# State-space layer and token mixer on one core: a third of the parameter chain to GpSimd, x's later rows issued earlier, two weight loads held back

## The chip, the cores and the metric

The kernel runs on one core of one Trainium2 chip. The metric is device time in microseconds (us) of one execution; lower is better. The engines are named as in the profile: PE (TensorE, with PEld for its weight loads), DVE (VectorE), ACT (ScalarE), POOL (GpSimd), and SP (SyncE), which issues most DMAs. POOL issues some DMAs too, on a queue of its own.

## The reference

A sequence x of 2048 tokens and 448 channels passes two blocks, each behind a layer norm whose scale and shift come from a conditioning vector c. Block A is a state-space convolution (S4D), computed by FFT; block B is a two-layer MLP over the token axis. Cut to what matters:

```python
def _A_ref(u, log_A_real, A_imag, C_real, C_imag, log_dt, D_skip):
    dt = jnp.exp(log_dt)
    A = -jnp.exp(log_A_real) + 1j * A_imag          # (448, 256)
    C = (C_real + 1j * C_imag) * dt[:, None]
    P = jnp.exp((A * dt[:, None])[:, :, None] * pos[None, None, :])
    K = 2.0 * jnp.einsum("dn,dnl->dl", C, P).real    # kernel, 448 x 2048
    y = jnp.fft.irfft(rfft(u_t, 2 * L) * rfft(K, 2 * L))[:, :, :L]
    return y + u * D_skip

mod = (silu(c) @ w_mod).reshape(1, 6, 1, 448)
sa, ca, ga, sb, cb, gb = ...                         # the six rows of mod
h = layernorm(x) * (1 + ca) + sa
x = x + ga * _A_ref(h, ...)
h = layernorm(x) * (1 + cb) + sb
x = x + gb * (w2.T @ gelu(w1.T @ layernorm(h) + b1) + b2)   # over tokens
```

## The kernel before

Everything is fp32. The convolution kernel K is built per step of 8 channels and 256 states: there are 56 steps (two for each of 28 groups of 16 channels), and the program runs them in sets of eight. A set begins with `window(s)`, s = 0, 8, 16, ..., 48, which does the part that needs the exponential's function table for all eight steps. Then come the eight steps themselves, which need the sine.

In `window`, for each of eight e: PE multiplies the exponent rows `lex` with the table `tab` into PSUM (`xe`, `xg`), and ACT takes their exponentials (`mag`). In each step, PE multiplies the phase rows `lph` (`st_phase`), ACT takes two absolute values and four sines (`ab`, `gs`, `xe`, `xg`), POOL makes the two halves of `G` (L679, L680), DVE the four parts of `E` (L681 to L687), and PE multiplies E and G into the kernel (`kg`, L710). For two later steps POOL makes `w` and `m` (L654, L656).

The rows `lex` and `lph` are parameters: from C, A and dt of each channel, magnitudes and phases are worked out, each split into two fp32r numbers `hl` (a rounded copy and the rest), and stored to a DRAM scratch `pars[q]`, from which SP loads a group's rows. q counts four blocks of 128 channels. Block 0 is done ahead of everything (`first_chain`), straight on 128 x 256 tiles. Blocks 1 to 3 are a Python generator, `chain(q)`: each `yield` ends one DVE instruction, and `more(n)` emits the next n of them at places that `WPACE` (in a set) and `pace` (in a step) name. So block 1's second half is emitted within the set of step 8, block 2's within the set of step 16, and block 3's along the steps behind. In those two sets DVE also empties PSUM for the FFT of u (`u_rows`, tile `yt`, L556): PE's `pu` waits for a free PSUM buffer, and the exponent matmuls are queued behind it.

x's rows come in three `x_load` calls, issued by POOL: rows 0 to 3 and 4 to 7 in `first_chain`, 8 to 15 behind step 0. `u_stats(r)` takes the mean and variance of row group r on DVE (L527, L528): 0 to 3 in the set of step 0, the others between the steps, by `late_rows`. All 16 are needed by ACT's `rs` (L462) and DVE's `nm` (L532) at the beginning of the set of step 8, and these by the normalised rows that `u_rows` multiplies.

The modulation rows 4 and 5 of `w_mod` are loaded late, into a part of `yks[1]` (`late_load`, called at steps 34 and 36 and read at steps 40 and 48).

The order of PE, ACT, DVE and POOL is the order of the code (a manual schedule). SP's order is made by a scheduler, which puts each DMA where its inputs and its buffer are expected to be ready. Each engine runs its queue in order. Behind step 55 come the inverse transform, the second layer norm and the MLP, in which PE is busy almost throughout.

Of the kernel before, what the change touches and what calls it, by code (L numbers as in the profile page):

```python
# [11 lines left out]
F32 = mybir.dt.float32  # L12
# [3 lines left out]
ALU = mybir.AluOpType  # L16
# [205 lines left out]
def tile_adaln_s4d_mixer(ctx, tc, i, out):  # L222
# [21 lines left out]
    with ExitStack() as es:  # L244
# [128 lines left out]
        def chain(q):  # L373


            w = N if q < 3 else P
            cr, ci, a, aim = (raws[q][nm][:, 0:w] for nm in ("A_C_real", "A_C_imag", "A_log_A_real", "A_A_imag"))
            xa, ya, s, t, u, ph, p64 = (
                qp.tile([P, N], F32, tag=nm, name=nm)[:, 0:w] for nm in ("xa", "ya", "s", "t", "u", "ph", "p64")
            )  # L380

            def split(src, to):
                hl = qp.tile([P, 2, N], F32R, tag="hl", name="hl", bufs=3)[:, :, 0:w]
                V.tensor_copy(hl[:, 0], src)
                yield
                tt(hl[:, 1], src, hl[:, 0].bitcast(F32), ALU.subtract)
# [10 lines left out]
            S.activation(xa, cr, AF.Abs, scale=0.5)  # L397
# [10 lines left out]
            ts(t, s, 2.0**-40, 2.0**80, ALU.is_lt, ALU.mult)  # L408
# [6 lines left out]
            ya = u  # L415
            yield from split(a, [(0, 1), (1, 1)])
            stt(s, t, -80 * math.log(2.0) / 2.0**80, s, ALU.mult, ALU.add)
            yield
            tt(s, ya, s, ALU.add)
            yield  # L420
            yield from split(s, [(2, 1)])
            yield "exponents"

            ts(ph, aim, dt4[:, q : q + 1], None, ALU.mult)
            yield
            ts(u, ph, MAGIC, MAGIC, ALU.add, ALU.subtract)
            yield
            tt(ph, ph, u, ALU.subtract)
            yield
            yield from split(ph, [(0, 0)])  # L430

            ts(u, ph, MAGIC / 128, MAGIC / 128, ALU.add, ALU.subtract)
            yield
            tt(p64, ph, u, ALU.subtract)
            yield
            yield from split(p64, [(1, 0)])

            ts(u, cr, 0.0, 0.5, ALU.is_ge, ALU.subtract)
            yield
            tt(xa, xa, u, ALU.mult)  # L440
            yield
            ts(u, ci, 0.0, 0.5, ALU.is_ge, ALU.subtract)
            yield
            stt(xa, xa, 0.5, u, ALU.add, ALU.mult)
            yield
            stt(xa, ph, 63.0, xa, ALU.mult, ALU.add)
            yield
            ts(u, xa, MAGIC, MAGIC, ALU.add, ALU.subtract)
            yield
            tt(xa, xa, u, ALU.subtract)  # L450
            yield
            yield from split(xa, [(2, 0)])
        def logs(root=False):

            if tmp:
# [43 lines left out]

        def late_load(k):  # L500
            a = (3456, 5376)[k - 4]
            wms[k] = late_room()[:, a : a + 4 * D].rearrange("p (q d) -> p q d", q=4)
            nc.sync.dma_start(wms[k], i["w_mod"][:, k * D : (k + 1) * D].rearrange("(q p) d -> p q d", p=PP))

# [353 lines left out]
        def first_chain():  # L858
# [79 lines left out]
            tt(xa, xa, u, ALU.subtract)  # L938
            store(ha, (0, 1), (1, 1))
            hl = split(G, p64)  # L940
            x_load(4, 4, G)
            direct(hl, lph, 64, 0)
            hc = split(V, xa)
            direct(hc, lph, 96, 0)
# [59 lines left out]
        def window(s):  # L1004
# [9 lines left out]
            for e in range(BATCH):  # L1014
                st_exp(s + e)

                if e + 1 < BATCH:
                    st_exponents(s + e + 1)
                else:
                    st_phase(s)  # L1020
                mellow()
                if s == 8 and e == 0:
                    tt(mod[1], mod[1], mod[2], ALU.mult)
                flush(dve)
                flush(act)
# [12 lines left out]
                if s in (8, 16):  # L1038
                    some(u_rows, rows, (1, 1, 1, 1, 1, 0, 0, 1)[e])
                elif s == 24 and e != 5:  # L1040
                    some(u_cols, cols, 1)

                if s == 32 and e == 2:
                    nc.sync.dma_start(t0, i["T0"].rearrange("p (j m) -> p j m", j=2))
                if s == 32 and e == 5:
                    pc_load(1)
                if s >= 40 and e == 2:
                    piece(False)
                if s >= 32 and e == 4:
                    piece(pieces[0] < NP, V)  # L1050
                if s == 0 and e in (4, 5):
                    st_mag2(e - 4)
                elif s and (e < 2 or s >= 32):
                    st_mag2(s + e)
                if s == 8 and e == 0:
                    u_norm(e + 2)
                if s == 0 and e == 3:
                    for r in range(4):
                        dsk_copy(r)
            if s == 0:  # L1060

                S.activation(one, one, AF.Sin)

        WPACE = [[0] * 8, [0, 2, 3, 4, 5, 5, 5, 5], [0, 5, 4, 4, 4, 4, 4, 4], [2] * 8]
        pace = [2] * 32
        mod_steps = {2: (1, 0), 3: (1, 1), 6: (2, 0, 1), 12: (0, 0), 13: (0, 1)}
        late_rows = {0: (4, 5), 3: (6, 7), 5: (8, 9, 10), 6: (11, 12, 13), 7: (14, 15)}
        tail = NHALF + 3  # L1070
        for s in range(tail):
            if s == 32:
# [402 lines left out]
```

## Time and profile before

| | |
|---|---|
| median of three runs | 683.14 us (681.51 to 683.85) |
| profiled execution | 685.58 us, span 683.7 us |
| PE busy | 614.2 us, 90% |
| PEld busy | 455.9 us, 67% |
| DVE busy | 446.5 us, 65% |
| ACT busy | 438.8 us, 64% |
| POOL busy | 267.6 us, 39% |
| granted TensorE clock | 0.970 |
| DMA | 121.14 MB, mean 177 GB/s |

Shares over the whole span say little here, since the stages have different bounds. On the time axis of the profile the parameters of block 0 and the set of step 0 take up to about 31 us, steps 0 to 7 up to 66, the set of step 8 up to 88, steps 8 to 15 up to 122, the set of step 16 up to 138, the set of step 32 lies at 221 to 235, the last step ends at about 344, and the MLP fills the rest. In a row of the order of time stand the start, the length, the engine, the line, the instruction with its output and inputs, and in brackets the engine's idle time before it with what ended that. A row of a table by stretches has the stretch, its length, and the busy time of PE, PEld, DVE, ACT and POOL (with counts), then the granted clock, the busy share of the DMA engines and GB/s.

### The profile page before, as it was taken

The numbers are of one execution on the slowest core, as the hardware profiler recorded it, in microseconds if no ns is written. First come the engines' busy times: TensorE is split into PE (matmuls) and PEld (weight loads), VectorE is DVE, ScalarE is ACT, GpSimd is POOL, SyncE is SP. The second block draws the span as 40 slices with busy tenths as digits, with TensorE's granted clock in tenths as the row PEclk, the third lists the DMA queues.
The fourth block names the chain that finished last, engine by engine and source line by source line (L and its number), as shares of the span: only waits on it lengthen the run. The fifth ranks groups of instructions, "written<-read, shape, count | busy, mean of one in ns | idle before, by whom it ended". The sixth has DMA issues, their size and how long they took to land. (4 is left out here: it accounts for less than half of the span.)

```text
span 683.7 us, 18268 instructions
## 1 busy us (share of the span) xinstructions
PE 614.2 (90%) x7180; PEld 455.9 (67%) x7180; DVE 446.5 (65%) x870; ACT 438.8 (64%) x880; POOL 267.6 (39%) x322
## 2 busy tenths in 40 slices
PE   0686789879988799999989899999999999999997
PEld 0354445435535456565667677779999999999996
DVE  7399798987689396885967587777422454443331
ACT  5787699879989799999945588877322322222220
POOL 6297468368369689898848100000000000000000
PEclk9999779989999899999999999999999999999999
DMA  8882455568896955344349799946674345555530
GB/s 182 237 181 75 174 173 188 194 208 261 264 288 191 206 124 179 99 138 131 99 140 314 231 256 257 243 127 198 167 213 135 95 141 168 165 162 170 167 119 28
DMA packets 106211, 121.14 MB, mean 177 GB/s; under 512 B 13098, under 2 KB 94718, under 8 KB 105998
## 3 DMA queue, kind: packets, MB, share of 16 engines
q1 hardware_dynamic: 104942, 114.72, 58.2%
q0 software_dynamic: 1184, 5.26, 3.4%
q8 instruction: 57, 0.93, 0.6%
q14 instruction: 28, 0.23, 0.1%
HBM read 84.59 MB, written 34.87 MB: 175 GB/s over the span
## 5 line engine op out<-in xcount | busy, mean ns | idle before, releaser
L207 ACT CAST whi<-w 128x896 fp32r<-128x896 f32 x64 | 59.7, 938 | 133.7 <-PE o L1442 84.7
L679 POOL TENSOR_TENSOR G<-mag,gs 128x512 f32<-128x512 f32 x56 | 72.1, 1288 | 66.9 <-ACT gs L675 66.7
L216 DVE TENSOR_TENSOR wlo<-w,whi 128x896 fp32r<-128x896 f32 x64 | 68.0, 1086 | 40.3 <-ACT whi L207 31.0
L1372 PE MATMUL acc<-h3h,whi 128*128 128x448 f32 x224 | 83.2, 372 | 1.2 <-ACT h3h L1277 1.2
L1374 PE MATMUL acc<-h3h,wlo 128*128 128x448 f32 x224 | 81.9, 366 | 0.0
L1373 PE MATMUL acc<-h3l,whi 128*128 128x448 f32 x224 | 81.6, 364 | 0.2 <-DVE h3l L1280 0.2
L1441 PE MATMUL o<-uh,whi 128*128 128x448 f32 x224 | 81.3, 363 | 0.0
L1443 PE MATMUL o<-uh,wlo 128*128 128x448 f32 x224 | 81.2, 362 | 0.0
L1442 PE MATMUL o<-ul,whi 128*128 128x448 f32 x224 | 80.6, 360 | 0.0
L710 PEld LDWEIGHTS kg<-E,G 128*32 128x32 f32 x3584 | 56.2, 114 | 31.5 <-issue 14.5
L627 PE MATMUL xg<-tab,lph 64*128 64x512 f32 x112 | 63.9, 572 | 12.6 <-DVE E L687 4.7
L680 POOL TENSOR_TENSOR G<-mag,gs 128x512 f32<-128x512 f32 x56 | 71.8, 1281 | 0.0
L710 PE MATMUL kg<-E,G 128*32 128x64 f32 x3584 | 66.1, 227 | 3.8 <-POOL G L680 1.7
L627 PE MATMUL xe<-tab,lph 64*128 64x512 f32 x112 | 63.7, 572 | 4.9 <-ACT gs L676 2.1
L1445 DVE SCALAR_TENSOR_TENSOR y<-o,b,mod 128x448 f32<-128x448 f32 x16 | 11.0, 685 | 80.3 <-PE o L1443 80.3
L656 POOL TENSOR_TENSOR m<-mag,w 128x512 f32<-128x512 f32 x56 | 59.7, 1065 | 4.4
L681 DVE TENSOR_TENSOR E<-m,xe 128x512 f32<-128x512 f32 x56 | 38.2, 682 | 26.0 <-ACT xe L674 21.9
L627 PE MATMUL xe<-tab,lex 64*128 64x512 f32 x56 | 31.1, 569 | 23.7 <-DMA lex<-wm 17.3
L1372 PEld LDWEIGHTS acc<-h3h,whi 128*128 128x128 f32 x224 | 42.4, 190 | 13.3 <-ACT h L1282 4.2
L1374 PEld LDWEIGHTS acc<-h3h,wlo 128*128 128x128 f32 x224 | 42.5, 190 | 3.3
L1373 PEld LDWEIGHTS acc<-h3l,whi 128*128 128x128 f32 x224 | 42.3, 189 | 3.4 <-DVE h3l L1280 0.5
L638 ACT ACTIVATE mag<-xe 128x512 f32<-128x512 f32 x56 | 35.5, 635 | 13.9 <-PE xe L627 5.7
(239 smaller groups left out, 1442.8 us busy)
## 6 DMA issues: line engine op xcount, KB each, us to landing
w<-in_B_w_dram SPq DMA_DIRECT2D x64, 224.0 KB
w<-in_B_w_dram SPq DMA_DIRECT2D x32, 448.0 KB
yu_d<-yt SPq DMA_DIRECT2D x16, 448.0 KB
yi<-yu_d SPq DMA_DIRECT2D x16, 448.0 KB
us_d<-uo SPq DMA_DIRECT2D x16, 448.0 KB
u<-us_d SPq DMA_DIRECT2D x32, 224.0 KB
v_d<-vt SPq DMA_DIRECT2D x32, 224.0 KB
vt<-v_d SPq DMA_DIRECT2D x14, 448.0 KB
```

The source lines that it names most:

```text
L207: self.nc.scalar.copy(hi, w)
L216: eng.tensor_tensor(lo, w, hi.bitcast(F32), ALU.subtract)
L627: T.matmul(out[k], lhs[r], rhs[r], start=start, stop=stop)
L679: G.tensor_tensor(Gt[:, 1], mg_, v32(sg), ALU.mult)
L680: G.tensor_tensor(Gt[:, 0], mg_, v32(cg_), ALU.mult)
L710: T.matmul(kgs[g][32 * q : 32 * q + 32, m], Gt[:, c, d], E[:, c, d], start=h == 0 and c == 0 and m == 0, stop=h == 1 and c == 1, skip_grou ...
L1372: nc.tensor.matmul(acc[f], hi[:, fs], h3h[:, r], start=r == 0, stop=False)
L1373: nc.tensor.matmul(acc[f], hi[:, fs], h3l[:, r], start=False, stop=False)
L1374: nc.tensor.matmul(acc[f], lo[:, fs], h3h[:, r], start=False, stop=r == 15)
L1441: nc.tensor.matmul(o, hi[:, ks], uh[kh][:, k], start=kh == 0 and k == 0, stop=False)
L1442: nc.tensor.matmul(o, hi[:, ks], ul[kh][:, k], start=False, stop=False)
L1443: nc.tensor.matmul(o, lo[:, ks], uh[kh][:, k], start=False, stop=kh == 1 and k == 6)
```

## The change

Three things are changed.

The phases' part of `chain(q)` for q = 1 and 2 goes from DVE to POOL (`E = G if q < 3 else V`). One instruction with two operations (63 times ph, plus xa) becomes two, so that 14 instructions leave DVE and 15 come to POOL in each of the two sets; the four sign instructions stay on DVE and come earlier. Block 3 stays on DVE with one instruction more.

x's rows 4 to 7 and 8 to 15 are issued by POOL within the set of step 0, behind the `m` of step 0 and of step 1. The statistics of rows 4 to 7 go to the end of that set, those of 8 to 15 into steps 2 to 6. Two modulation matmul groups go from steps 2 and 3 to 3 and 4.

`late_load` first writes one column of its room on DVE, and the load waits for that write, so it can't start before steps 34 and 36.

```diff
-            def split(src, to):
+            def split(src, to, eng=V):
...
+            E = G if q < 3 else V
+            r = ya
+            def turn(v):
+                E.tensor_scalar(r, v, MAGIC, MAGIC, ALU.add, ALU.subtract)
+                yield
+                E.tensor_tensor(v, v, r, ALU.subtract)
+                yield
+            E.tensor_scalar(ph, aim, dt4[:, q : q + 1], None, ALU.mult)
+            yield
+            yield from turn(ph)
+            yield from split(ph, [(0, 0)], E)
             ts(u, cr, 0.0, 0.5, ALU.is_ge, ALU.subtract)
...
-            stt(xa, ph, 63.0, xa, ALU.mult, ALU.add)
...
+            E.tensor_scalar(r, ph, MAGIC / 128, MAGIC / 128, ALU.add, ALU.subtract)
+            yield
+            E.tensor_tensor(p64, ph, r, ALU.subtract)
+            yield
+            yield from split(p64, [(1, 0)], E)
+            E.tensor_scalar(r, ph, 63.0, None, ALU.mult)
+            yield
+            E.tensor_tensor(xa, xa, r, ALU.add)
+            yield
+            yield from turn(xa)
+            yield from split(xa, [(2, 0)], E)
...
         def late_load(k):
+            V.memset(late_room()[:, a : a + 1], 0.0)
...
             hl = split(G, p64)
-            x_load(4, 4, G)
...
                 if s == 0 and e in (4, 5):
                     st_mag2(e - 4)
+                    x_load((4, 8)[e - 4], (4, 8)[e - 4], G)
...
             if s == 0:
+                for r in range(4, 8):
+                    u_stats(r)
...
-        WPACE = [[0] * 8, [0, 2, 3, 4, 5, 5, 5, 5], [0, 5, 4, 4, 4, 4, 4, 4], [2] * 8]
+        WPACE = [[0] * 8, [2, 2, 3, 4, 5, 5, 5, 5], [0, 5, 4, 4, 4, 4, 4, 4], [2] * 8]
-        mod_steps = {2: (1, 0), 3: (1, 1), 6: (2, 0, 1), 12: (0, 0), 13: (0, 1)}
-        late_rows = {0: (4, 5), 3: (6, 7), 5: (8, 9, 10), 6: (11, 12, 13), 7: (14, 15)}
+        mod_steps = {3: (1, 0), 4: (1, 1), 6: (2, 0, 1), 12: (0, 0), 13: (0, 1)}
+        late_rows = {2: (8,), 3: (9, 10), 4: (11, 12), 5: (13,), 6: (14, 15)}
...
-            if s == 0:
-                x_load(8, 8, G)
```

The order of the instructions shows what moves. First POOL, from block 0's last cast to the end of step 0; `xt` holds x's rows, and a row of 32x1792 x4 is rows 4 to 7, of 32x3584 x4 rows 8 to 15. Before:

```order
L869 CAST wm_79<-p_186 128x256
L870 TENSOR_TENSOR wm_79<-p_186,wm_79 128x256
L305 DMA xt<-in_A_u_dram 32x1792 x4
L477 COPY dsk<-dskr 1x112 x4
L654 TENSOR_TENSOR w<-mag 128x16
L656 TENSOR_TENSOR m_329<-mag,w 128x512
L654 TENSOR_TENSOR w<-mag 128x16
L656 TENSOR_TENSOR m_343<-mag,w 128x512
L679 TENSOR_TENSOR G<-mag,gs 128x512
L680 TENSOR_TENSOR G<-mag,gs 128x512
L305 DMA xt<-in_A_u_dram 32x3584 x4
```

And the same place on POOL after:

```order
L875 TENSOR_TENSOR wm_79<-p_186,wm_79 128x256
L481 COPY dsk<-dskr 1x112 x4
L659 TENSOR_TENSOR w<-mag 128x16
L661 TENSOR_TENSOR m_325<-mag,w 128x512
L305 DMA xt<-in_A_u_dram 32x1792 x4
L659 TENSOR_TENSOR w<-mag 128x16
L661 TENSOR_TENSOR m_343<-mag,w 128x512
L305 DMA xt<-in_A_u_dram 32x3584 x4
L684 TENSOR_TENSOR G<-mag,gs 128x512
```

Rows 4 to 7 are issued later, behind the first `m`, and rows 8 to 15 earlier, ahead of the first `G`.

Next DVE in the set of step 8, from block 1's last magnitude to the first `E` of step 8; `yt` is the emptying of PSUM that PE's `pu` waits for. Before (the rows from p to the sign instructions left out):

```order
L386 TENSOR_TENSOR hl<-s,hl 128x256
L424 TENSOR_SCALAR ph<-A_A_imag,dt_172 128x256
L426 TENSOR_SCALAR u<-ph 128x256
L556 TENSOR_TENSOR yt<-pu,mod_105 128x448 x2
L428 TENSOR_TENSOR ph<-ph,u 128x256
L384 CAST hl<-ph 128x256
L386 TENSOR_TENSOR hl<-ph,hl 128x256
L432 TENSOR_SCALAR u<-ph 128x256
L434 TENSOR_TENSOR p_414<-ph,u 128x256
L556 TENSOR_TENSOR yt<-pu,mod_105 128x448 x2
```

And DVE after, from the same instruction to the first `E`:

```order
L386 TENSOR_TENSOR hl<-s,hl 128x256
L734 TENSOR_TENSOR ks<-ks,dsk 128x4
L561 TENSOR_TENSOR yt<-pu,mod_105 128x448 x4
L436 TENSOR_SCALAR u<-A_C_real 128x256
L438 TENSOR_TENSOR xa<-xa,u 128x256
L440 TENSOR_SCALAR u<-A_C_imag 128x256
L442 SCALAR_TENSOR_TENSOR xa<-xa,u 128x256
L561 TENSOR_TENSOR yt<-pu,mod_105 128x448 x4
L686 TENSOR_TENSOR E<-m_979,xe 128x16x32
```

Between the sets of `yt` only the four sign instructions are left; the fourteen others now stand on POOL, between the set's last `m` and the first `G` of step 8. The set of step 16 changes in the same way.

Last SP around the late weight loads (`yk<-in_w_mod`), in and behind the set of step 32. Before:

```order
L779 DMA si<-in_SI_dram 128x512
L503 DMA yk_3470<-in_w_mod_dram 112x4x448
L774 DMA u<-us_d 128x448
L503 DMA yk_3470<-in_w_mod_dram 112x4x448
L785 DMA yk_1115<-in_SI_dram 128x384
L774 DMA u<-us_d 128x448
L613 DMA lex_146<-pars_59 32x256
L617 DMA lex_146<-pars_59 64x1x256
```

And SP after, from the last of the next set's `lex` loads on:

```order
L618 DMA lex_149<-pars_59 32x256
L622 DMA lex_149<-pars_59 64x1x256
L779 DMA u<-us_d 128x448
L784 DMA si<-in_SI_dram 128x512
L846 DMA v_d<-vt 128x2x224
L618 DMA lph_144<-pars_59 32x256
L622 DMA lph_144<-pars_59 64x1x256
L790 DMA yk_1117<-in_SI_dram 128x384
L508 DMA yk_3473<-in_w_mod_dram 112x4x448
```

The first of the two loads now stands behind the four `lex` pairs, and the second follows some transfers later, each waiting for its write on DVE.

More of the change, by code (lines that the diff above doesn't have):

```diff
@@ L380, in chain @@
             )
-            def split(src, to):
+            def split(src, to, eng=V):
                 hl = qp.tile([P, 2, N], F32R, tag="hl", name="hl", bufs=3)[:, :, 0:w]
-                V.tensor_copy(hl[:, 0], src)
+                eng.tensor_copy(hl[:, 0], src)
                 yield
-                tt(hl[:, 1], src, hl[:, 0].bitcast(F32), ALU.subtract)
+                eng.tensor_tensor(hl[:, 1], src, hl[:, 0].bitcast(F32), ALU.subtract)
                 for k, v in to:
@@ L418, in chain @@
             yield
-            tt(s, ya, s, ALU.add)
+            tt(s, u, s, ALU.add)
             yield
@@ L422, in chain @@
             yield "exponents"
-            ts(ph, aim, dt4[:, q : q + 1], None, ALU.mult)
-            yield
[L426 to L436, printed above, removed]
+            E = G if q < 3 else V
[6 more added lines that the diff above has]
+            E.tensor_scalar(ph, aim, dt4[:, q : q + 1], None, ALU.mult)
+            yield
+            yield from turn(ph)
+            yield from split(ph, [(0, 0)], E)
             ts(u, cr, 0.0, 0.5, ALU.is_ge, ALU.subtract)
@@ L445, in chain @@
             yield
-            stt(xa, ph, 63.0, xa, ALU.mult, ALU.add)
+            E.tensor_scalar(r, ph, MAGIC / 128, MAGIC / 128, ALU.add, ALU.subtract)
             yield
-            ts(u, xa, MAGIC, MAGIC, ALU.add, ALU.subtract)
+            E.tensor_tensor(p64, ph, r, ALU.subtract)
             yield
-            tt(xa, xa, u, ALU.subtract)
+            yield from split(p64, [(1, 0)], E)
+            E.tensor_scalar(r, ph, 63.0, None, ALU.mult)
             yield
-            yield from split(xa, [(2, 0)])
+            E.tensor_tensor(xa, xa, r, ALU.add)
+            yield
+            yield from turn(xa)
+            yield from split(xa, [(2, 0)], E)
         def logs(root=False):
```

1 line of the change is left out of this document (removed).

## The prediction

> **What bounds the kernel now.** I read busy time by stretches first, one stretch for each place that the change touches, then the order of time of each engine there, then who waited for whom.
>
> ```profile
> 33.00:64.00 31.00, 24.47 (x450) 14.29 (x450) 30.43 (x55) 26.42 (x54) 30.05 (x33) 0.94 0.62 150
> 69.00:88.00 19.00, 14.99 (x191) 8.28 (x184) 14.41 (x38) 11.88 (x25) 7.23 (x10) 0.80 0.56 188
> 125.00:138.00 13.00, 10.88 (x171) 6.03 (x167) 11.71 (x29) 11.24 (x24) 2.68 (x4) 1.00 0.64 234
> 222.00:236.00 14.00, 10.30 (x202) 6.30 (x205) 3.91 (x9) 10.49 (x21) 10.70 (x17) 0.79 1.03 232
> ```
>
> After the stretch and its length stand the busy times of PE, PEld, DVE, ACT and POOL, then granted clock, DMA share, GB/s. Steps 0 to 7 (33 to 64): DVE and POOL are both full, 30.4 and 30.1 of 31 us. Set of step 8 (69 to 88) and set of step 16 (125 to 138): DVE is the busiest or nearly, POOL almost idle. Set of step 32 (222 to 236): DMA is full and every engine has gaps. The stages behind 236 us have none of the changed work, so I take a gain ahead of them as passed on to the end.
>
> **Steps 0 to 7.** In order of time, DVE, ACT, POOL:
>
> ```profile
> 32.96 0.69 DVE L681 TENSOR_TENSOR E<-m,xe 128x512 f32<-128x512 f32 x1 [11.46 <-ACT xe L674]
> 57.47 0.59 DVE L527 BATCH_NORM_STATS2 st<-xt 128x6 f32<-128x448 f32 x1
> 58.20 0.59 DVE L527 BATCH_NORM_STATS2 st<-xt 128x6 f32<-128x448 f32 x1
> 68.15 0.31 ACT L462 ACTIVATE rs<-mv,small_t 128x16 f32<-128x16 f32 x1 [2.38 <-DVE mv L528]
> 68.74 0.18 DVE L532 TENSOR_TENSOR nm<-rs 128x16 f32<-128x16 f32 x1 [0.62 <-ACT rs L463]
> 35.89 2.00 POOL L305 DMA_DIRECT2D xt<-in_A_u_dram  x4
> ```
>
> One row's statistics take 58.20 - 57.47 = 0.73 us. Rows 4 to 7 leave this stretch for DVE's idle 11.46 us ahead of 32.96: 4 x 0.73 = 2.9 us. The last rows' statistics now stand ahead of step 7's products, so rs no longer makes DVE wait: 0.62. POOL's issue at 35.89 goes ahead of its first G, into idle time: 2.0. As DVE is the later one, nm could start 3.5 us earlier.
>
> Against that stand the transfers. Rows 4 to 7 (4 x 224 KB) now go behind POOL's first m instead of ahead of it, and rows 8 to 15 (4 x 448 KB = 1.84 MB) behind its second m, ahead of the first G, instead of at 35.89. There they meet:
>
> ```profile
> 23.32 2.04 SPq L884 DMA_DIRECT2D pars<-wm  x4
> 27.79 0.37 SPq L613 DMA_DIRECT2D lph<-pars  x1
> 34.28 0.42 ACT L397 ACTIVATE xa<-A_C_real 128x256 f32<-128x256 f32 x1
> 34.50 0.46 PE L627 MATMUL xe<-tab,lph 64*128 64x512 f32 x1 [1.96 <-ACT xg L677]
> 42.37 0.68 DVE L681 TENSOR_TENSOR E<-m,xe 128x512 f32<-128x512 f32 x1
> 39.00 0.60 ACT L674 ACTIVATE xe<-xe 128x512 f32<-128x512 f32 x1
> 22.00:28.00 6.00, 5.75 (x15) 2.97 (x13) 0.00 (x0) 5.57 (x12) 1.29 (x2) 1.00 0.88 304
> 28.00:36.00 8.00, 5.21 (x21) 3.13 (x21) 2.88 (x5) 7.97 (x17) 2.55 (x3) 0.97 0.66 168
> q1 hardware_dynamic: 104942, 114.72, 58.2%
> q0 software_dynamic: 1184, 5.26, 3.4%
> ```
>
> The lph load at 27.79 reads what the stores at 23.32 write, and step 2's matmul at 34.50 reads lph. If the 1.84 MB go wholly ahead of those stores, at 304 GB/s, lph comes 6.0 us later; if behind, not at all. ACT's xa at 34.28, whose input SP issues between the two, is exposed in the same way, and all of ACT queues behind it. Step 2's sine ran at 39.00 to 39.60 and its reader at 42.37: 2.8 us of slack. Worst case 6.0 - 2.8 = 3.2 late, of which DVE wins back rows 6 and 7 (1.45) and 0.62: +1.1. Ends: -3.5 and +1.1. The mean packets of POOL's queue are 4.4 KB against 1.1 KB of SP's, so I lean to part of the delay: -1.8.
>
> The Trainium skill's page DMA: Bandwidth & Descriptors (Queues, rings and completion order) says that an engine takes turns between queues packet by packet; with larger packets on POOL's queue this would give the +1.1 end, 679.0 in all, against 675.6 by my lean. No run yet shows which.
>
> Ahead of step 0, in the first set:
>
> ```profile
> 21.60 0.79 PE L627 MATMUL xg<-tab,lex 64*128 64x512 f32 x1 [3.52 <-DMA lex<-wm]
> ```
>
> This wait for lex loses the competition of rows 4 to 7, but the lph of step 0, which SP issues behind it and which ends the same set, gains it. Ends: -3.5 (the wait gone) and +3.5 (the same wait moved to lph); I take -0.5, near the middle, because the transfers change places rather than go away. Rows 4 to 7 themselves: POOL issues them near the start of DVE's 11.46 idle us, of which 2.9 are now used, so they have about 8.5 us to land. Two modulation matmul groups move one or two steps later and the pace of the set of step 8 starts two instructions earlier: the same work in steps with the same bound, at 0. Together: **-2.3**.
>
> **The set of step 8.** The steps that leave DVE, first and last, then who waits for DVE, and POOL:
>
> ```profile
> 80.56 0.34 DVE L424 TENSOR_SCALAR ph<-A_A_imag,dt 128x256 f32<-128x256 f32 x1
> 88.86 0.42 DVE L386 TENSOR_TENSOR hl<-xa,hl 128x256 fp32r<-128x256 f32 x1
> PE y L748 <- DVE yt L556: 1.8, 2, 1.3
> PE pu L553 <- DVE yt L556: 1.1, 2, 0.7
> 91.38 1.27 POOL L679 TENSOR_TENSOR G<-mag,gs 128x512 f32<-128x512 f32 x1 [14.13 <-ACT gs L675]
> 12.75 0.52 POOL L869 CAST wm<-ph 128x256 fp32r<-128x256 f32 x1 [2.48 <-DVE ph L927]
> 13.35 0.77 POOL L870 TENSOR_TENSOR wm<-ph,wm 128x256 fp32r<-128x256 f32 x1
> 74.30 1.62 POOL L543 TENSOR_SCALAR xt<-xt,rs,nm 128x448 f32<-128x448 f32 x2
> ```
>
> Fourteen DVE instructions of 0.28 to 0.43 leave this set, 5.0 us. PE waited for DVE's yt 1.8 + 1.1 = 2.9 us; the exponent matmuls and ACT's mag queue behind that. So the gain lies between 0 and 5.0, bounded in practice by PE's 2.9: I take **-2.0**, since the next paragraph eats some.
>
> POOL gets fifteen instructions: 7 two-input x 0.77, 3 casts x 0.52, 5 scalar x 0.46 (1.62/2 x 256/448) = 9.3 us, behind the set's last m and ahead of G at 91.38. The cover is POOL's 14.13 idle us; if it were gone, G would be late and ACT would wait for its gs buffers. DVE supplies xa half-way through the set, before POOL's eleventh instruction. The stores that these fifteen feed are read from step 16 on, with steps 8 to 15 between.
>
> DVE and POOL disturb each other:
>
> ```profile
> 44.76 1.98 DVE L408 TENSOR_SCALAR t<-s 128x256 f32<-128x256 f32 x1
> 102.98 0.48 DVE L408 TENSOR_SCALAR t<-s 128x256 f32<-128x256 f32 x1
> 127.78 1.27 DVE L417 SCALAR_TENSOR_TENSOR s<-t,s 128x256 f32<-128x256 f32 x1
> 77.90 0.41 DVE L417 SCALAR_TENSOR_TENSOR s<-t,s 128x256 f32<-128x256 f32 x1
> ```
>
> The long ones stand beside a POOL tensor instruction, the short ones do not (an m beside the 1.27). Six such DVE instructions remain beside the moved chain; at most 0.77 each is 4.6 us, almost what left.
>
> The Trainium skill, SBUF — State Buffer (SBUF: two separate sides), states this as an exclusive lock that also takes DVE instructions with two SBUF inputs; the 1.27 against 0.41 agrees. By it alone the set would gain some 0.4 us, and the whole change come to 678.2 (rival 2).
>
> **The set of step 16**, the same chain:
>
> ```profile
> PE pu L553 <- DVE yt L556: 1.5, 2, 1.0
> PE y L748 <- DVE yt L556: 0.6, 1, 0.6
> 141.17 0.69 DVE L681 TENSOR_TENSOR E<-m,xe 128x512 f32<-128x512 f32 x1 [1.16 <-ACT xe L674]
> 141.65 1.27 POOL L679 TENSOR_TENSOR G<-mag,gs 128x512 f32<-128x512 f32 x1 [12.89 <-ACT gs L675]
> ```
>
> PE's waits are 2.1, and DVE already waits 1.16 for ACT at the end, so less is to be had: between 0 and 2.1, **-1.2**. POOL's cover is 12.89 against 9.3. The third group's chain stays on DVE with one instruction of 128x128 more: 0.3 us, hidden, at 0.
>
> **The weight loads.**
>
> ```profile
> 223.34 0.34 SPq L503 DMA_DIRECT2D yk<-in_w_mod_dram  x1
> 229.14 0.50 PE L627 MATMUL xe<-tab,lex 64*128 64x512 f32 x1 [2.97 <-issue]
> 231.67 0.60 ACT L638 ACTIVATE mag<-xe 128x512 f32<-128x512 f32 x1 [0.91 <-issue]
> ```
>
> Two loads of 784 KB, the first at 223.34 and one right after, go into a full DMA (share 1.03 above), and PE, then ACT, stand still 2.97 and 0.91 us for nothing that the profile shows. I read it as instructions fetched late through the same DMA engines. A memset on DVE now releases each load at steps 34 and 36 (cost 0 to 1.5 us each, as 1.98 against 0.48; I take 0, DVE has gaps there), and on SP they stand behind lex and u loads, which so come earlier. Behind the waiting load SP holds si and v_d transfers for one step at most. Its readers come at steps 40 and 48. Ends: 0 and -3.9. The si and u loads that also fill DMA there stay, so I take the half, **-2.0**.
>
> **Sum.** -2.3 - 2.0 - 1.2 - 2.0 = -7.5 us. The profiled execution took 685.58 us (span 683.7), the median is 683.14: I forecast 683.1 - 7.5 = **675.6**. What a measurement can tell from no change is 0.3%, 2.0 us.
>
> **Rivals.**
> 1. The x transfers hold up SP's: first term +1.1 instead of -2.3, 679.0. For it: packet sizes and the lph chain; against it: DMA is at 0.66 from 28 to 36.
> 2. DVE and POOL block each other: both sets gain 0.4 and 0.2, 678.2. For it: 1.98 against 0.48. With rival 1, 681.6: no change.
> 3. The loads' hold does nothing, the stall comes from si and u loads: 677.6.
> 4. Slower: POOL's chain outlasts its cover. At P us per instruction G is late by 15P - 14.1 and 15P - 12.9, and the steps behind it wait; both sets' gains are then gone, and with the other two terms the sum is 30P - 27.0 - 4.3. It turns positive at 1.04 and reaches +2 at 1.11; at G's own 1.27 it is +6.8, 689.9. Against it: G is twice as wide, and the narrow rows say 0.46 to 0.77, so it would take blocking by DVE at nearly every instruction.
> 5. All terms at their good ends, -3.5 - 3.5 - 2.9 - 2.1 - 3.9 = -15.9: 667.2.
>
> **Chances.** Forecast (673 to 678) 0.46, rival 1 0.14, rival 2 0.10, rival 3 0.08, rivals 1 and 2 together 0.10, rival 4 0.05, towards 5 (below 673) 0.07. Faster 0.46 + 0.14 + 0.10 + 0.08 + 0.07 = 0.85, same 0.10, slower 0.05. The range from 669.5 to 682.0 takes in rivals 1 to 3 and their mixture and leaves out rival 4 and the last few us of 5.
>
> **What would show it.** nm near 66 instead of 68.74; no wait of ACT's rs for mv; lph of step 2 without a DMA wait; the first G of the sets of 8 and 16 still released by ACT's gs and not by POOL; PE's waits for yt under 1 us in each set; no gap of 3 us on PE in the set of step 32. The prediction is wrong if POOL's moved instructions run over 1.0 us each, or if ACT's xa of step 0 waits for its transfer for more than 4 us.

## The result and the profile after

The change made the kernel slower: 693.51 us median (692.43 to 694.68) against 683.50 (681.51 to 685.73) of the kernel before beside it, ratio 1.015 with the interval 1.012 to 1.0179. The profiled execution has a span of 692.9 us against 683.7.

The times at which ACT starts `ab`, the first instruction of a step, show where. From these rows of the order of time (before, then after) I work out all differences below:

```profile
38.02 0.60 ACT L664 ACTIVATE ab<-xe 128x512 f32<-128x512 f32 x1
```

```profile
45.08 0.60 ACT L669 ACTIVATE ab<-xe 128x512 f32<-128x512 f32 x1 [2.23 <-PE xe L632]
```

Step 2 is 45.08 - 38.02 = 7.06 us late. The same difference for the other steps, in the profile of each kernel that was run (+ is later than before, in us; the ratio is that of the timed runs):

| kernel | step 2 | 7 | 8 | 16 | 18 | 19 | 31 | 33 | 40 | 55 | ratio (95%) |
|---|---|---|---|---|---|---|---|---|---|---|---|
| before starts at | 38.02 | 58.63 | 87.78 | 138.06 | 147.67 | 153.67 | 217.87 | 239.65 | 274.89 | 340.48 | |
| changed | +7.06 | +5.42 | +2.21 | +1.38 | +1.69 | +5.68 | +5.95 | +6.68 | +8.96 | +8.84 | 1.015 (1.012-1.0179) |
| e11 changed, again | +5.65 | +4.00 | +0.71 | -0.13 | +0.18 | +4.04 | +4.34 | +1.06 | +3.26 | +3.09 | 1.0105 (1.0074-1.0137) |
| e1 x rows alone | +7.00 | +5.40 | +2.90 | +3.86 | +3.14 | +2.82 | +2.85 | -0.80 | -0.78 | -0.79 | 1.0034 (1.0004-1.0063) |
| e2 chain alone | +1.12 | +1.12 | +1.07 | +0.25 | +0.57 | +4.59 | +4.90 | +1.59 | +1.62 | +1.62 | 1.0036 (1.001-1.0063) |
| e3 hold alone | -0.04 | +0.42 | -0.56 | +0.34 | -0.40 | -0.70 | -0.69 | -2.82 | +0.53 | +0.48 | 1.0005 (0.9972-1.0038) |
| e4 chain, hold | +1.12 | +1.14 | +0.23 | -0.64 | -0.33 | +2.85 | +3.13 | -0.54 | +2.14 | +1.89 | 1.0057 (1.003-1.0085) |
| e5 rows 4-7 | -0.62 | +4.49 | +3.03 | +3.28 | +2.55 | +2.21 | +2.25 | +0.96 | +0.94 | +0.91 | 1.0055 (1.0027-1.0084) |
| e6 chain, own queue | -0.30 | -0.56 | -1.73 | +2.41 | +7.19 | +6.14 | +8.07 | +4.67 | +4.70 | +4.66 | 1.0114 (1.0083-1.0145) |
| e7 chain left out | -0.28 | -0.55 | -2.12 | -3.63 | -4.07 | -4.60 | -1.68 | +0.02 | +0.11 | -0.05 | 0.9993 (0.9969-1.0018) |
| e8 = e5 + e6 | -0.61 | +4.39 | +1.79 | +5.87 | +10.79 | +9.77 | +13.61 | +15.53 | +15.54 | +15.56 | 1.0175 (1.0134-1.0216) |
| e9 rows 8-15 on SP | -0.66 | +10.85 | +7.36 | +8.97 | +8.94 | +9.17 | +9.16 | +6.92 | +6.94 | +6.88 | 1.0078 (1.0051-1.0105) |
| e10 rows 4-7, late statistics | -1.23 | +2.46 | +0.27 | +2.16 | +2.14 | +2.39 | +2.54 | -0.76 | -0.73 | +1.14 | 1.0013 (0.9978-1.0048) |
| e12 hold, quarter loads | +0.02 | +0.05 | +0.55 | +0.30 | +0.30 | +0.81 | +0.80 | -2.27 | -1.08 | -1.23 | 1.0003 (0.9973-1.0033) |
| e13 scalars on DVE | -0.14 | +0.52 | -0.82 | -1.66 | -1.54 | -0.46 | -0.18 | -0.21 | -0.21 | -0.23 | 1.0004 (0.9977-1.0032) |
| e14 more work on an idle POOL | -0.62 | -0.22 | -0.03 | +1.10 | +1.08 | +1.00 | +1.00 | -0.18 | -0.19 | -0.19 | one run |

The differences come from one profile of each kernel, the ratios from its timed runs. Read along a row: where the number jumps, time is lost or won. The changed kernel loses in steps 0 to 2, wins in the set of step 8, loses between steps 18 and 19, and again towards step 40.

Two cautions on single rows. Between steps 31 and 33 most rows fall by 1 to 4 us, because before itself stood still there for 2.97 us in its profile. And rows differ where nothing was changed: of the kernels that leave the set of step 16 as it was, e14 loses 1.52 us in it (steps 15 to 16), e9 and e10 about 1.4, and e3, e5 and e12 nothing. So a jump of under 1.5 us in one row is no finding by itself.

The stretches of before, a few us later to stand at the same work (the columns as there):

```profile
38.00:70.00 32.00, 24.61 (x451) 14.20 (x451) 28.28 (x52) 25.24 (x51) 24.64 (x25) 1.00 0.41 114
75.00:94.00 19.00, 15.20 (x244) 8.98 (x240) 12.01 (x23) 12.89 (x24) 17.80 (x25) 0.89 0.55 200
130.00:144.00 14.00, 11.71 (x111) 5.76 (x107) 9.14 (x17) 12.60 (x25) 12.97 (x17) 1.00 0.62 228
230.00:244.00 14.00, 11.73 (x168) 7.46 (x166) 4.26 (x9) 11.39 (x22) 10.33 (x16) 0.72 0.40 128
```

In the sets of steps 8 and 16 POOL, the fifth busy time, is now nearly full (17.80 of 19 and 12.97 of 14 us, where it had 7.23 of 19 and 2.68 of 13), and DVE, the third, is now below PE and ACT in both.

**Steps 0 to 2.** SP's transfers are late. First the waits of the changed kernel there (total, times, longest), then the DMA queues from 28 to 36 us (packets, MB, share of the 16 engines), of the changed kernel and of before:

```profile
ACT xa L397 <- DMA A_C_real<-in_A_C_real_dram: 5.8, 1, 5.8
DVE s L399 <- ACT ya L398: 5.3, 1, 5.3
PE xe L632 <- DVE s L399: 8.0, 1, 8.0
PE xg L632 <- DMA lph<-pars: 2.2, 1, 2.2
```

```profile
q0 software_dynamic: 169, 1.68, 81.5%
q1 hardware_dynamic: 234, 0.42, 21.4%
```

```profile
q1 hardware_dynamic: 1083, 1.33, 65.2%
```

POOL's queue (q0) carries rows 8 to 15 and moves 1.68 MB in those 8 us; SP's queue (q1) is left with 0.42 MB, where it moved 1.33 before. Two things come late from it. ACT waits 5.83 us for the real part of C, all its queue behind that, and DVE behind ACT. And SP's two loads of `lph` for step 2 wait 4.2 and 4.7 us for the stores to `pars` that they read. SP's own waits, the two loads and the matmul on the second of them, after; then the second load before:

```profile
SPq L618 <- DMA pars<-wm: 4.2, 1, 4.2
SPq L622 <- DMA pars<-wm: 4.7, 1, 4.7
33.56 0.33 SPq L618 DMA_DIRECT2D lph<-pars  x1
38.67 0.61 SPq L622 DMA_DIRECT2D lph<-pars  x1
43.33 0.76 PE L632 MATMUL xg<-tab,lph 64*128 64x512 f32 x1 [2.24 <-DMA lph<-pars]
```

```profile
28.26 0.61 SPq L617 DMA_DIRECT2D lph<-pars  x1
```

The second load is issued 10.41 us later. The `ab` of step 2, at 45.08, then waits 2.23 us for PE: what came last there was `lph`, not ACT. (PE's wait of 8.0 us is put down to DVE's `s` here; in e1 the same wait, 7.8 us, is put down to `lph`.) The loss of 7 us is partly won back by step 7 and in the set of step 8, where ACT's `rs` no longer waits for the statistics; it is now DVE that waits for `rs`:

```profile
71.39 0.29 ACT L466 ACTIVATE rs<-mv,small_t 128x16 f32<-128x16 f32 x1
71.97 0.18 DVE L537 TENSOR_TENSOR nm<-rs 128x16 f32<-128x16 f32 x1 [1.90 <-ACT rs L467]
```

**Sets of steps 8 and 16.** POOL's chain in the set of step 16, first to fourth and last instruction, and the G behind it, after:

```profile
130.68 1.09 POOL L431 TENSOR_SCALAR ph<-A_A_imag,dt 128x256 f32<-128x256 f32 x1
131.86 1.08 POOL L426 TENSOR_SCALAR ya<-ph 128x256 f32<-128x256 f32 x1
133.02 0.89 POOL L428 TENSOR_TENSOR ph<-ph,ya 128x256 f32<-128x256 f32 x1
133.98 0.40 POOL L384 CAST hl<-ph 128x256 fp32r<-128x256 f32 x1
...
142.94 0.74 POOL L386 TENSOR_TENSOR hl<-xa,hl 128x256 fp32r<-128x256 f32 x1
143.64 1.27 POOL L684 TENSOR_TENSOR G<-mag,gs 128x512 f32<-128x512 f32 x1
```

From 130.68 to 143.64 are 12.96 us (12.73 in the set of step 8) where the prediction had 9.3; G follows without an idle moment.

**Steps 18 to 19.** SP's store of the chain's last result, its loads of `yi` behind that, and PE's matmul on `yi`, after; then SP and PE before:

```profile
143.70 0.32 SPq L389 DMA_DIRECT2D pars<-hl  x1
147.09 2.16 SPq L577 DMA_DIRECT2D yi<-yu_d  x4
153.38 3.32 PE L586 MATMUL pu<-yi,s 128*128 128x448 f32 x4 [3.69 <-DMA yi<-yu_d]
```

```profile
141.03 1.92 SPq L572 DMA_DIRECT2D yi<-yu_d  x4
147.92 2.61 PE L581 MATMUL pu<-yi,s 128*128 128x448 f32 x3
```

The store waits for POOL; five transfers of `lex` stand between it and the four `yi` loads. `yi` is issued 6.06 us later, and PE waits 3.69 us for it.

**Sets of steps 32 and 40.** PE's idle of 2.97 us in the set of step 32 is gone, and one of 2.60 us stands in the set of step 40, behind the held loads (after):

```profile
250.79 0.35 SPq L508 DMA_DIRECT2D yk<-in_w_mod_dram  x1
259.74 0.38 SPq L508 DMA_DIRECT2D yk<-in_w_mod_dram  x1
270.28 0.58 PE L753 MATMUL y<-wc,ks 64*64 64x64 f32 x9 [2.60 <-issue]
```

In this one execution the granted clock was also at half from 236 to 246 us (the column behind POOL's):

```profile
236.00:246.00 10.00, 9.70 (x94) 6.21 (x96) 6.01 (x12) 7.12 (x13) 6.32 (x8) 0.50 0.27 73
```

### The profile page after: what moved, and what is told of

Its sections match the earlier page's. It is cut to its first block, busy times and chain, and to the rows that moved or that the text cites. A ratio compares the mean times of both kernels' runs of the same rounds, so it can differ in the third digit from the quotient of the medians.

```text
span 692.9 us, 18281 instructions
## 1 busy us (share of the span) xinstructions
PE 614.3 (89%) x7180; PEld 456.7 (66%) x7180; DVE 438.6 (63%) x845; ACT 437.7 (63%) x880; POOL 291.1 (42%) x352
## 5 line engine op out<-in xcount | busy, mean ns | idle before, releaser
L1450 DVE SCALAR_TENSOR_TENSOR y<-o,b,mod 128x448 f32<-128x448 f32 x16 | 10.9, 683 | 80.3 <-PE o L1448 80.3
L669 ACT ACTIVATE ab<-xe 128x512 f32<-128x512 f32 x56 | 34.0, 607 | 24.9 <-PE xe L632 18.7
```

## The experiments

### The three parts, one by one (e1 to e4)

My theory T1 was that each loss sits at the part whose work stands there; the rival T2 that the late x transfers shift all that follows; T3 is the sum of the prediction. Each kernel is before with a part of the diff:

```diff
 e1:  x_load(4, 4) and x_load(8, 8) behind st_mag2(0), st_mag2(1); late_rows, mod_steps as changed
 e2:  chain(q) with E = G if q < 3 else V; WPACE as changed
 e3:  + V.memset(late_room()[:, a : a + 1], 0.0)
 e4:  e2 and e3
```

e1: 

> The kernel before with the second part alone: x's rows 4 to 15 issued within the first set, their statistics and two modulation groups moved with them. Theory T1 (each loss sits at the part whose work stands there): steps 0 to 2 come about 7 us later, some 5.4 us of it is left at step 7, and the whole run is 4 to 6 us slower; ACT's xa of the second group waits for its transfer for about 5 us. Rival T2 (one cause: the late transfers shift everything behind them against the DMA queues, and the later losses at step 19, step 33 and the set of step 40 follow from that shift): about 9 us slower, with the waits at steps 19 and 33 present here too. Rival T3 (the prediction's own sum): 1 to 3 us faster.

e2: 

> The kernel before with the first part alone: the phases' instructions of the next channels on GpSimd in the sets of steps 8 and 16. Theory T1: the set of step 8 gains about 3.2 us and that of step 16 0.5 us, and 4.0 us are lost at step 19, where SP's loads of yi stand behind the last store of GpSimd's chain: in all within 1 us of before. T2: the loss at step 19 is not there without the late x transfers, so 3 to 4 us faster. T3: 3 us faster, with GpSimd's chain of 9.3 us; T1 has it at 12.7 us.

e3: 

> The kernel before with the third part alone: a memset on VectorE releases each of the two late weight loads. Theory T1: PE's idle of 2.97 us in the set of step 32 is gone and comes back as 2.6 us or so in the set of step 40, and step 33 starts some 1.5 us later against step 32, so 2 to 4 us slower. T2: the idle at step 40 comes from the shift alone, so this kernel is 1 to 2 us faster. T3: 2 us faster.

e4: 

> The changed kernel without its second part (x's rows 4 to 15 are issued as before; the other two parts stay). T1: the parts add up, so the loss of the changed kernel of about 9 us falls by the 5.4 us of the second part, to 3 to 4 us slower than before. T2: everything behind step 7 is well, so 4 to 6 us faster than before. T3: 5 us faster.

The table above bears T1 out site by site. e1 alone has the delay (+7.00 at step 2, +5.40 at step 7) and none of the loss at step 19; e2 alone has the loss at step 19 (+0.57 to +4.59) without a late transfer ahead of it; T2 falls. In e1 step 8 comes 2.5 us nearer again, so most of the 3.2 us that the changed kernel won in the set of step 8 come with the second part. Whether the statistics won them or the set had slack for a late start isn't separated: e10, with the statistics of rows 8 to 15 where before had them, starts step 7 late by 2.46 and wins 2.2 there too. With the chain that set wins 0.05 us by step 8 (e2) and 0.91 (e4): T1, which had 3.2 there, was wrong on that. In the timed runs, by the ratios, e1 is 2.3 us slower (T1 had 4 to 6), e2 2.5 slower (T1: within 1), e3 no different (T1: 2 to 4 slower), e4 3.9 slower (T1: 3 to 4). T1 has the places right, and the sizes only for e4.

Both kernels with the hold have the idle in the set of step 40, neither without it has one of 2 us there (e2 has 1.23). Of e3 and of e4:

```profile
261.60 0.44 PE L749 MATMUL y<-wc,ks 64*64 64x64 f32 x10 [2.82 <-issue]
```

```profile
263.37 0.39 PE L753 MATMUL y<-wc,ks 64*64 64x64 f32 x9 [2.88 <-issue]
```

But the idle of 2.97 us of before in the set of step 32 isn't in e1's or e2's profile either, though their loads were not held. Of the eleven profiles with the loads unheld, three have it: before, e7 (2.57) and e8 (3.52). It was no fixed cost of the kernel.

### The x rows (e5, e9, e10)

```diff
 e5:   if e == 4: x_load(4, 4, G)        # rows 8 to 15 after step 0, as before
       late_rows = {3: (8,), 4: (9, 10), 5: (11, 12, 13), 6: (14, 15)}
 e9:   x_load((4, 8)[e - 4], (4, 8)[e - 4], (G, nc.sync)[e - 4])   # else as e1
 e10:  e5 with late_rows = {5: (8, 9, 10), 6: (11, 12, 13), 7: (14, 15)}
```

e5: 

> Of the second part only rows 4 to 7: they are issued behind the first m of the first set, their statistics stand at its end, and rows 8 to 15 are issued after step 0 as before (their statistics in steps 3 to 6). Theory A (the 1.84 MB of rows 8 to 15, put ahead of SP's transfers of parameters, made the 7 us): step 2 is within 1.5 us of before, the set of step 8 gains the 2.5 us that it gained with the whole second part, so 2 to 3 us are gained by step 16 and the run is about 2 us faster. Rival A2 (rows 4 to 7 alone already push SP's transfers back): step 2 at least 3 us later, the run no faster than before. Rival A3 (the gain of 2.5 us in the set of step 8 only paid back the delay, since ACT and GpSimd are as full as VectorE in steps 0 to 7): no delay and no gain, within 1 us of before.

e9: 

> The second part alone, with one word changed: rows 8 to 15 are issued by SP, behind the parameters' transfers and the modulation weight that stand in its queue, instead of by GpSimd. Place, bytes and statistics stay those of the second part. Theory A (the 7 us come from two queues sharing the DMA engines, of which GpSimd's with its larger packets gets most): step 2 within 1.5 us of before instead of 7 us later; the rows still land in time for the statistics from step 2 or 3 on, so 2 us of the gain in the set of step 8 show and the run is 1 to 3 us faster than before. Rival A4 (the bytes are the trouble, whichever queue carries them): steps 1 and 2 come 5 us or more later here too.

e10: 

> e5 with the statistics of rows 8 to 15 left in steps 5, 6 and 7 as before, so that they do not ask for the rows before these land at about 54 us. Theory A: no wait of 5.9 us, steps 1 to 7 0.6 us earlier or better, VectorE 2.9 us lighter in steps 0 to 3, so nm 1 to 3 us earlier and the run 1 to 3 us faster. Rival A3 (ACT and GpSimd set the pace of steps 0 to 7, so nothing is gained but 0.6 us): no change.

Without rows 8 to 15 on POOL's queue, step 2 is on time (-0.62, -0.66, -1.23): theory A holds for the delay, and rivals A2 and A4 fall. e9 has the bytes and the place in the code of e1, but SP sends the rows behind the parameters, at 33.07 instead of 23.65. So it shows that the delay goes when these bytes come last, and doesn't tell the sharing of two queues from the order of the bytes; for the sharing stand the packets and MB of the two queues above. The gain that A promised did not come: e5 is 3.8 us slower than before and e9 5.4. What I had wrong is when the rows land. In e5 they are issued at 35.27, in e9 at 33.07, and DVE's first statistics of them wait till 54 us (e5, then e9):

```profile
54.79 0.63 DVE L527 BATCH_NORM_STATS2 st<-xt 128x6 f32<-128x448 f32 x1 [5.91 <-DMA xt<-in_A_u_dram]
```

```profile
53.71 0.63 DVE L527 BATCH_NORM_STATS2 st<-xt 128x6 f32<-128x448 f32 x1 [10.30 <-DMA xt<-in_A_u_dram]
```

In e5 these four transfers took 11.1 to 17.9 us from issue to landing, in before 4.9 to 10.9; the two loads of modulation weights of 784 KB each, which SP issues at 32.86 and POOL at 42.58, move in the same stretch. Before asked for the rows at 56.7 us, behind their landing. e10 asks as late as that and has no such wait, but wins nothing from the lighter DVE: at step 7 it is 2.46 us late, partly from a modulation weight that now lands late (`pm` waited 2.74 us for it). A3, that nothing is to be had there, fits it best: 1.0013 (0.9978 to 1.0048), where A had 1 to 3 us faster.

### The chain (e6, e7, e8, e13, e14)

```diff
 e6:   (G if eng is G else nc.sync).dma_start(pars[q][v, k], ...)     # else as e2
 e7:   G.memset(hl) and three stores in place of the fifteen instructions   # else as e2
 e8:   e5 and e6
 e13:  the five tensor_scalar of a chain with ts (DVE) instead of E         # else as e2
 e14:  before, + memset, 3 tensor_scalar, 2 tensor_tensor on POOL behind st_mag2(1)
```

e6: 

> The first part alone, with GpSimd's results stored by GpSimd's own DMA queue instead of SP's. Theory D (SP's queue waits at the last of these stores for GpSimd's last hl, and the loads of yi stand behind it): the 4.0 us between steps 18 and 19 are gone; GpSimd's chain grows by its three issues at about 0.5 us each, so the sets of steps 8 and 16 end up to 1 us later; in all within 1 us of before, against 2.4 us slower with SP's queue. Rival D2 (yi waits for bandwidth or for other loads on SP): the loss at step 19 stays above 3 us.

e7: 

> The first part alone with GpSimd's fifteen instructions of each chain left out (a memset of one buffer and its three stores stand for them, so the phases of the second and third group are not computed): VectorE loses its fourteen instructions and GpSimd gains next to none. Theory C (VectorE was not what set the end of these two sets: PE's and VectorE's exchange of pu, yt and y is a ring that VectorE's other instructions merely filled): the set of step 8 gains less than 1.5 us, that of step 16 less than 1 us. Rival C2 (the gain was there, and GpSimd's instructions beside VectorE's ate it): the set of step 8 gains 3 us or more and that of step 16 1 to 2 us, so 4 us faster in all. Either way the loss at step 19 is gone.

e8: 

> e5 and e6 together: rows 4 to 7 moved, the chain on GpSimd with its own queue. By theories A and D the two add: 2 us faster than before, give or take 1. If GpSimd in steps 0 to 16 is the bound (its chain of 12.7 us and three issues ahead of the set's first G), the chain takes back 1 us of e5's gain.

e13: 

> The first part alone, with the five scalar instructions of each chain (about 1.08 us each on GpSimd, 0.29 on VectorE) left on VectorE and only the subtractions, additions and casts on GpSimd. If GpSimd's chain blocks VectorE by its length: GpSimd's part falls from 12.7 us to about 8, its last store comes about 4 us earlier, the loss of 4.0 us at step 19 shrinks to 1 at most, the set of step 8 gains about 1 us, and the run is 0 to 2 us faster than before. Rival: the blocking comes from the two-input instructions that stay on GpSimd, and the two engines now wait for each other at every step: no gain in the set of step 8, and the loss at step 19 stays above 2 us.

e14: 

> The kernel before with six more GpSimd instructions on 128x256 in the first set, while VectorE stands idle: a memset, two tensor_scalar with two immediates, one with one, two subtractions or additions. Their results are used by nothing. If 1.08 us is GpSimd's own time for two immediates: 1.0 to 1.1 us here too, 0.87 with one, 0.73 for the two-input ones. If VectorE's instructions beside them made them long: 0.5 to 0.6 us.

*Where the gain went (e7).* With POOL's instructions left out the same fourteen DVE instructions are worth 3.35 us by step 16 and 4.3 by step 19 (-0.28 to -3.63 and -4.60). With them they are worth 0.87 by step 16 in e2 (+1.12 to +0.25) and 1.76 in e4. So the work on POOL took back about half to three quarters of what DVE's relief brought, which speaks for rival C2 and against theory C; it is one profile against two. C2's sizes are not met: the set of step 8 wins 1.57 us (C: under 1.5, C2: 3 or more), that of step 16 wins 1.17, and in all e7 is level with before (0.9993) where C2 had 4 us. Three rows of DVE's groups in the set of step 8 show the mechanism, of before and then of e2:

```profile
L438 DVE TENSOR_SCALAR u<-A_C_real 128x256 f32<-128x256 f32 x1 | 0.3, 289 | 0.0
L442 DVE TENSOR_SCALAR u<-A_C_imag 128x256 f32<-128x256 f32 x1 | 0.3, 294 | 0.0
L444 DVE SCALAR_TENSOR_TENSOR xa<-xa,u 128x256 f32<-128x256 f32 x1 | 0.4, 425 | 0.0
```

```profile
L436 DVE TENSOR_SCALAR u<-A_C_real 128x256 f32<-128x256 f32 x1 | 0.7, 731 | 0.0
L440 DVE TENSOR_SCALAR u<-A_C_imag 128x256 f32<-128x256 f32 x1 | 0.5, 507 | 0.0
L442 DVE SCALAR_TENSOR_TENSOR xa<-xa,u 128x256 f32<-128x256 f32 x1 | 0.9, 906 | 0.0
```

289 became 731 ns, 425 became 906 ns beside POOL's chain; in e7, without it, they took 282 and 425. The four sign instructions together are 1.2 us longer in this set and 0.7 in the set of step 16. The Trainium skill states a lock between DVE and POOL in SBUF — State Buffer (SBUF: two separate sides); the rows agree with it. Here instructions with one input became longer too.

*Where step 19 lost (e6).* With POOL's own queue, `yi` is issued at 143.47 instead of 145.96 in e2 and PE's wait for it is gone; step 19 comes 1.05 us nearer instead of 4.0 farther. Theory D holds. But the queue cost POOL more than it saved: each of three stores takes 0.3 us of wait and 0.6 of issue, and once, in the set of step 16, POOL waited for a buffer whose store had not left:

```profile
140.73 0.40 POOL L384 CAST hl<-p 128x256 fp32r<-128x256 f32 x1 [2.91 <-DMA pars<-hl]
142.22 0.60 POOL L389 DMA_DIRECT2D pars<-hl  x1 [0.30 <-POOL hl L386]
148.77 1.28 POOL L683 TENSOR_TENSOR G<-mag,gs 128x512 f32<-128x512 f32 x1
```

The first G of that set came at 148.77 instead of 142.51 in e2, and step 18 was 7.19 us late: now the chain did outlast its cover. In all e6 is 7.8 us slower than before, where I had expected within 1. e8 has this and e5's late rows together, was expected 2 us faster, and is 12 us slower, more than either.

*POOL's own time (e14).* Beside an idle DVE (nothing on it from 21.5 to 32.3 us):

```profile
24.68 2.26 POOL L1057 TENSOR_SCALAR zp<-zph 128x256 f32<-128x256 f32 x2
27.02 0.88 POOL L1058 TENSOR_SCALAR zp<-zph 128x256 f32<-128x256 f32 x1
27.98 0.73 POOL L1059 TENSOR_TENSOR zt<-zph,zp 128x256 f32<-128x256 f32 x1
```

2.26 / 2 = 1.13 us with two immediates, 0.88 with one, 0.73 with two tensors: POOL's instructions are as long as this by themselves. DVE was delayed by POOL; POOL was by DVE hardly: in the set of step 16 two of the seven two-input ones took 0.89 and 0.97.

*Scalars back on DVE (e13).* The set of step 8 wins 1.34 us, the loss between steps 18 and 19 falls from 4.02 to 1.08, as expected of the shorter chain. The chain took 9.6 us there, not the 8 expected, since the two engines wait for each other at some steps:

```profile
80.17 0.73 POOL L428 TENSOR_TENSOR ph<-ph,ya 128x256 f32<-128x256 f32 x1 [2.66 <-DVE ya L426]
```

In all 1.0004 (0.9977 to 1.0032): the mended chain is as fast as before, not faster. That it beats e2 (1.001 to 1.0063) isn't shown, as the intervals overlap.

### The weight loads, and the whole once more (e12, e11)

```diff
 e12:  + V.memset(late_room()[:, a : a + 1], 0.0); V.memset(wms[k][:, 1:4], 0.0)
       - nc.sync.dma_start(wms[k], ...)  + nc.sync.dma_start(wms[k][:, 0:1], ...)
 e11:  the changed kernel
```

e12: 

> The third part alone, with only a quarter of each late weight loaded (the other three quarters are set to zero on VectorE, so two modulations are computed from a part of their weights). Theory H (the two loads of 784 KB fill the DMA engines, so that a packet of instructions for PE comes late and PE stands still for 2.6 to 2.9 us, wherever the loads are put): no idle of PE over 1 us put down to issue in the sets of steps 32 and 40, and 2 to 3 us faster than before. Rival H2 (the stall belongs to the place in the instruction stream, or to the si and u loads): an idle of 2.5 us or more stays in the set of step 40.

e11: 

> The changed kernel once more, unaltered, on the chip of the other runs of this call. If the parts add up (e1 +2.3, e4 +3.9 in the medians, ratios 1.0034 and 1.0057): 691 to 692, ratio 1.006 to 1.011, and the half granted clock of the set of step 32 in the first profile (236 to 246 us, some 4 us lost) is not there in a second one. If parts act on each other: ratio 1.013 or more again, with the half clock in the set of step 32 again.

e12 has no idle of PE put down to issue of even 1 us in the sets of steps 32 and 40. All four profiles with the full loads held (the changed kernel, e3, e4, e11) have 2.3 to 2.9 us there. That speaks for theory H as to the cause, the loads' bytes, and against rival H2, with one profile of e12. The DMA engines from 252 to 262 us were busy at 0.93 with the full loads and 0.69 with a quarter (e3, then e12):

```profile
252.00:262.00 10.00, 7.18 (x225) 5.14 (x222) 9.31 (x17) 8.85 (x19) 8.69 (x9) 1.00 0.93 243
```

```profile
252.00:262.00 10.00, 9.27 (x295) 6.66 (x297) 9.43 (x17) 9.53 (x22) 8.45 (x9) 1.00 0.69 203
```

Its size does not hold: 2 to 3 us were expected and 1.0003 was measured. Its profile is 1.23 us ahead at step 55; the span ends 1.4 us behind that of before.

e11 repeats the losses at steps 2, 19 and 40 (+5.65; 0.18 to 4.04; 1.06 to 3.26), and not the half clock. From step 31 to 33 the first profile took 22.51 us, this one 18.50, so 4.0 of the first profile's 9.2 us were that clock, which the runs don't tie to the change. Its ratio 1.0105 lies within what the parts add up to (1.0034 and 1.0057) and its interval touches that of the first comparison, 1.012 to 1.0179. I take the change as some 7 to 10 us slower.

No version beat the kernel before.

## Why the prediction was wrong, step by step

The forecast was -7.5 us, and +10.0 and +7.2 were measured (the changed kernel, e11). Three terms failed. Steps 0 to 7, -2.3, had the right wait at too small a price: +2.3 in the timed e1. The two sets, -3.2, left out the place of POOL's last store in SP's queue, which cost 4.0 us at step 19, and about half to three quarters of their gain was lost beside POOL's instructions, which made DVE's longer: +2.5 in the timed e2. The weight loads, -2.0, priced a stall that most profiles don't have: no change in e3.

- **Steps 0 to 7, -2.3; bad end +1.1.** Failed; +5.4 at step 7. The mechanism was named (rival 1: POOL's larger packets take the turns, and ACT's `xa` is "exposed in the same way"), the size was not. The bound of 6.0 us took 1.84 MB at 304 GB/s and SP's chain as one transfer; the queue moved 1.68 MB in 8 us, 210 GB/s, and several transfers of SP follow from one another: the second load of `lph` was issued 10.41 us later, not 6.0. The 2.8 us of slack, taken between ACT's sine and DVE's reader, didn't help, because ACT itself stood still for 5.83 us at `xa` and PE at `lph`. The test set there, a wait over 4 us, is met. The rule of the Trainium skill's page DMA: Bandwidth & Descriptors (Queues, rings and completion order) agrees with the trace in the window shown: 169 and 234 packets, not far from turn and turn about, carry 1.68 and 0.42 MB. Leaning to a part of the delay was wrong, but the +1.1 of the whole was too small as well.
- **The statistics, -3.5 within that.** Half right: `rs` no longer waits for `mv`, and step 8 comes 2.5 us nearer than step 7 (e1). "As DVE is the later one" failed: `nm` came at 71.97 and not near 66, behind the delay, and DVE waited 1.90 us for ACT's `rs`. The first set, -0.5: -1.07 measured.
- **The set of step 8, -2.0.** Failed: 0.05 (e2) and 0.91 (e4). The price of DVE's relief alone was not far off: in e7 the sets of steps 8 and 16 won 1.57 and 1.17, against -2.0 and -1.2. Rival 2 had the direction, POOL's instructions lengthen DVE's: 3.35 us without them by step 16, 0.87 (e2) and 1.76 (e4) with them.
- **POOL's chain, 9.3 us.** Mis-sized: 12.7 to 13.0. The five scalar instructions were scaled from a 128x448 row to 0.46 us; they take 0.88 to 1.13 by themselves (e14), 5.2 us for the five instead of 2.3. Another 1.0 us lies between the fifteen, where the sum had none. Of the fifteen only four are over 1.0 us, so the prediction's test of POOL's instructions is not met, and rival 4 came to little: the first G of the set of step 16 stood at 142.51 in e2, 0.9 us behind the 141.65 of before.
- **The set of step 16, -1.2, and "the stores that these fifteen feed are read from step 16 on".** The set won 0.55 in e2 and then 4.0 were lost. The sentence looked at who reads the data and not at what stands behind the store in SP's queue. Rival 4 looked for the slower side at G; it was at `yi`.
- **The weight loads, -2.0.** Wrong as a cost: a stall of this kind stands in three of the eleven profiles with the loads unheld. Held, it moved to the set of step 40 and was there in all four. e3: 1.0005.
- **"A gain is passed on."** Not shown, and doubtful: e7 was 4.60 ahead at step 19 and level at step 33. Its profile shows half-clock stretches on the way; whether they came of being early or by chance is open.

## What to carry to other kernels

A transfer that is issued earlier on a second queue is not free because its engine is idle: list the small transfers of the first queue in that window, and give the large packets most of the bandwidth when you price them. Moving work to a slower engine moves its stores too, and whatever stands behind them in a queue that runs in order; and where the two engines block each other, the work that leaves one comes back as longer instructions on it. A stall seen in one profiled execution is no price until a second execution or kernel shows it again.

## What the runs showed of the hardware

- An idle of PE that nothing in the profile explains (2.3 to 3.5 us) appears 2 to 8 us after the second of two large loads is issued, in seven profiles: the four with the loads held and before, e7 and e8. It isn't there in eight others with the same loads unheld, nor with loads of a quarter of their bytes (e12). In all seven a packet of the instruction queue q8 started between 0.3 us before PE fell idle and 0.9 us after. In before PE fell idle at 226.17 us, and the one packet that started from 226.0 to 226.5 took 1.35 us (16.9% of 16 engines for half a microsecond):

```profile
q8 instruction: 1, 0.02, 16.9%
```

  That instructions were late is argued from this, not shown: such packets also stand where nothing stalls (four in e12 from 252 to 266 us). The Trainium skill, Runtime: NRT & Kernel Launch (Instruction fetch mechanics), holds the fetch to be mostly hidden; if the reading is right, these rows are an exception to it, with the DMA engines nearly full.
- On POOL a 128x256 fp32 instruction with one tensor and two immediates took 1.13 us, longer than one with two tensors (0.73). On DVE the first kind took 0.29 (`u<-ph` in the set of step 8 of before).
- Rows 8 to 15, issued at 33 to 35 us, were waited for until about 54 (e5, e9). In e9 SP's queue was full from 33 to 41 us (1.66 MB), with a weight load of 784 KB just ahead of the rows in it.
